# A gated linear recurrence and a cosine MLP on one core: every chunk in pairs, two tokens to a partition, and one written order of steps

## The chip, the cores and the metric

The kernel runs on one core of a Trainium2 chip. The metric is the device time of one execution in microseconds. Times given as a span come from one execution taken by the hardware profiler, from the first instruction to the last.

The engines: PE (TensorE) multiplies matrices into PSUM, eight banks of 512 float32 columns; DVE (VectorE), ACT (ScalarE) and POOL (GpSimd) work elementwise; SP (SyncE) issues DMAs, and ACT can as well. Each has its own queue and takes its instructions in order. They wait for one another by semaphores.

## The reference

```python
f = 1.0 / (1.0 + np.exp(-f_logit))              # B, H, S, D = 4, 8, 768, 48
state = np.zeros((B, H, D, D))
for t in range(S):
    state = f[:, :, t, :, None] * state + np.einsum('bhd,bhe->bhde', k[:, :, t], v[:, :, t])
    y[:, :, t] = np.einsum('bhd,bhde->bhe', q[:, :, t], state)
x = y.transpose(0, 2, 1, 3).reshape(B * S, H * D)       # 3072 x 384
h = x @ w_in                                    # w_in 384 x 2048
out = (h * np.cos(h)) @ w_out                   # w_out 2048 x 384
```

Inputs and output are float32.

## The kernel before

The 768 steps of a batch are cut into six chunks of 128 tokens, 24 chunks in all. Within a chunk the recurrence is written as masked attention; a state goes from chunk to chunk.

A chunk goes through these steps, which the text calls by these names. Loads of f, k, q and v (`load`, L396 and L399). *decay*: exp and log of f on ACT (L422, L437), running sums over the tokens on PE (L448 to L461), and their exponentials b and bi on ACT (L468). *Products* q b and k bi (L482, mostly POOL), v cast to bf16 (L389). Transposes of both products on PE (L511, L515) and their copy qkt out of PSUM (L525). *Scores* on PE (L541, L550), masked by DVE (am, L554). *Outer product* of keys and v on PE (L570, L575), added to the state by DVE (st, L584) and decayed (sz, L590). y from the state (L600) and from the scores (inner y, L607 and L612), copied out (yb, L525), transposed on PE (L630) and copied (xT, L525).

The MLP works on units of 128 or 256 tokens. *h* is x by w_in on PE (L651), into two banks; ACT takes the cosine (L658), DVE the product with h (gT, L661). *o* multiplies gT by w_out on PE in four quarters of four matmuls (L671), ACT or DVE copy the sum out (ot, L674), SP stores it (L682, L685). The weights come in by eight loads of 768 KB and are cast to bf16 (L389).

Exp and log are in one table of ACT, the cosine in another; ACT_TABLE_LOAD changes them (L737, L658). So decay is done for groups of chunks (`GROUPS`), seven in all.

The first four chunks (`NPAIR = 4`) are loaded as pairs of tokens: a partition takes tokens 2p and 2p+1, in pieces of 384 bytes, and two groups of four heads stand on the two halves of the partitions. The matmuls of these chunks take a form of their own (L448 to L454, L511, L541, L570, L607), in which a v padded with zeros (vp) keeps the halves apart. The other twenty put one token on a partition, in pieces of 192 bytes.

The order of the steps isn't written out. `Plan.run` takes every step with an assumed cost for each engine that may do it and a priority (`PR`), and puts next what can start first. It gives each step its engine, its buffer (`Slots`) and its banks (`Banks`): h may take banks 0 to 5, scores 2 to 7, single banks 2 to 7. A PSUM tile has two banks.

Of the kernel before, what the change touches and what calls it, by code (L numbers as in the profile page):

```python
# [9 lines left out]
F32 = mybir.dt.float32  # L10
# [3 lines left out]


class Slots:


    def __init__(self, aps, name):
        self.aps, self.name = aps, name  # L20
        self.free_at = [0.0] * len(aps)
        self.held = [False] * len(aps)
        self.last, self.now = [[] for _ in aps], [[] for _ in aps]

    def best(self):
        free = [(t, i) for i, t in enumerate(self.free_at) if not self.held[i]]
        return min(free) if free else None

    def take(self, i):
        self.held[i] = True  # L30
        self.last[i], self.now[i] = self.now[i], []

    def users(self, i):
        return self.last[i]

    def used(self, i, t, o):
        self.free_at[i] = max(self.free_at[i], t)
        self.now[i].append(o)

    def drop(self, i):  # L40
        self.held[i] = False

    def ap(self, i):
        return self.aps[i]


class Banks:


    def __init__(self, base, size, starts, name):  # L50
        self.base, self.size, self.starts, self.name = base, size, starts, name

    def best(self):
        b, out = self.base, None
        for k, s in enumerate(self.starts):
            r = range(s, s + self.size)
            if any(b["held"][i] for i in r):
                continue
            c = (max(b["free"][i] for i in r), k, s)
            if out is None or c < out:  # L60
                out = c
        return None if out is None else (out[0], out[2])

    def take(self, s):
        for i in range(s, s + self.size):
            self.base["held"][i] = True
            self.base["last"][i], self.base["now"][i] = self.base["now"][i], []

    def users(self, s):
        return sum((self.base["last"][i] for i in range(s, s + self.size)), [])  # L70

    def used(self, s, t, o):
        for i in range(s, s + self.size):
            self.base["free"][i] = max(self.base["free"][i], t)
            self.base["now"][i].append(o)

    def drop(self, s):
        for i in range(s, s + self.size):
            self.base["held"][i] = False

    def ap(self, s):
        t = self.base["tiles"][s // 2]
        return t if self.size == 2 else t[:, (s % 2) * 512:(s % 2) * 512 + 512]


class Val:


    def __init__(self, pool=None, ap=None):
        self.pool, self._ap, self.slot = pool, ap, None  # L90
        self.writers, self.uses, self.parts = [], 0, []
# [6 lines left out]
    @property  # L98
    def ap(self):
        return self._ap if self.pool is None else self.pool.ap(self.slot)  # L100


class Part:
    def __init__(self, whole, cut):
        self.whole, self.cut, self.writers = whole, cut, []
# [6 lines left out]
class Op:  # L112
    __slots__ = ("seq", "eng", "fn", "prio", "table", "deps", "vals", "alloc", "start", "end",
                 "lat", "waiting", "after", "grp", "dma", "name", "prior", "cost")


class Plan:


    SEM = 60.0  # L120
    PE_LAT = 180.0
    TABLE = 1290.0
    WINDOW = 60.0

    def __init__(self):
        self.ops = []

    def op(self, name, eng, fn, reads=(), writes=(), prio=0.0, table=None, lat=0.0, grp=None,
           dma=None):
        o = Op()  # L130
        o.name, o.eng, o.fn, o.prio, o.table = name, eng, fn, prio, table
        o.lat, o.grp, o.dma, o.prior = lat, grp, dma, []
        o.seq, o.deps, o.alloc, o.vals, o.after = len(self.ops), set(), [], [], []
        for v in reads:
            o.deps.update(v.writers)
            if isinstance(v, Val):
                for p in v.parts:
                    o.deps.update(p.writers)
        for v in writes:
            w = getattr(v, "whole", v)  # L140
            if w.pool is not None:
                o.alloc.append(w)
            if v.writers:
                o.deps.add(v.writers[-1])
        for v in list(reads) + list(writes):
            v = getattr(v, "whole", v)
            if v.pool is not None and v not in o.vals:
                o.vals.append(v)
                v.uses += 1
        for v in writes:  # L150
            v.writers.append(o)
        self.ops.append(o)
        return o

    def run(self):
        free = dict.fromkeys(("PE", "ACT", "DVE", "POOL", "SP"), 0.0)
        table, lock, bus, hot, pe_end = None, None, 0.0, 0.0, 0.0
        left = {}
        for o in self.ops:
            o.waiting = len(o.deps)  # L160
            for d in o.deps:
                d.after.append(o)
            if o.grp is not None:
                left[o.grp] = left.get(o.grp, 0) + 1
        ready = [o for o in self.ops if not o.waiting]
        order, n = [], len(self.ops)
        while len(order) < n:
            cand = []
            for o in ready:
                at, pe = 0.0, "PE" in o.eng  # L170
                for d in o.deps:
                    t = d.end + (0.0 if pe and d.eng == "PE" else self.SEM)
                    if pe and d.eng == "PE":
                        t = d.end - d.lat
                    at = max(at, t)
                ok = True
                for v in o.alloc:
                    if v.slot is not None:
                        continue
                    b = v.pool.best()  # L180
                    if b is None:
                        ok = False
                        break
                    at = max(at, b[0] + self.SEM)
                if not ok:
                    continue
                pick = None
                for e, cost in o.eng.items():
                    if e == "ACT" and lock is not None and o.grp != lock and o.table is not None:
                        continue  # L190
                    s = max(at, free[e])
                    sw = self.TABLE if e == "ACT" and o.table not in (None, table) else 0.0
                    if pick is None or s + cost + sw < pick[0]:
                        pick = (s + cost + sw, s, e, cost)
                if pick is not None:
                    cand.append((pick[1], o.prio, o.seq, o, pick[2], pick[3]))
            assert cand, "no op can be placed: " + str(
                [(o.name, o.prio, lock, o.grp, [v.pool.name for v in o.alloc]) for o in ready])
            first = min(cand, key=lambda c: c[:3])
            best = min((c for c in cand if c[4] == first[4] and c[0] <= first[0] + self.WINDOW),  # L200
                       key=lambda c: (c[1], c[0], c[2]))
            s, _, _, o, e, cost = best
            if e == "ACT" and o.table is not None:
                if o.table != table:
                    s += self.TABLE
                table = o.table
                if o.grp is not None:
                    left[o.grp] -= 1
                    lock = o.grp if left[o.grp] else None
            for v in o.alloc:  # L210
                if v.slot is None:
                    v.slot = v.pool.best()[1]
                    v.pool.take(v.slot)
                    o.prior += v.pool.users(v.slot)
            o.cost = cost
            if e == "PE":
                hot *= math.exp((pe_end - s) / 2500.0)
                if hot < 0.5:
                    cost *= 1.9
                hot = 1.0 - (1.0 - hot) * math.exp(-cost / 2500.0)  # L220
                pe_end = s + cost
            o.start = s
            free[e] = s + cost
            if o.dma is not None:
                bus = max(s + cost + 700.0, bus) + o.dma
                o.end = bus + 1250.0
            else:
                o.end = s + cost + (self.PE_LAT if e == "PE" else 55.0 if e in ("ACT", "DVE") else 0.0)
                o.lat = o.end - s - cost
# [20 lines left out]
NPAIR = 4  # L250
# [519 lines left out]
```

## Time and profile before

| | |
|---|---|
| time, median of 3 runs | 227.56 us (226.14 to 229.81) |
| profiled execution, span | 225.4 us |
| busy: PE, DVE, ACT, POOL | 187.4, 138.2, 137.8, 71.8 us |
| instructions of PE (matmuls) | 1976 |
| mean granted clock of TensorE | 0.970 |
| moved by DMA | 30.20 MB, mean 134 GB/s |
| packets under 512 B | 92480 of 99158 |

The profiled execution has no time of its own beside the runs; its span is 2.2 us below their median. A line of the profile names the line of the kernel, the engine and the operation, then what is written and read. Busy times of PE are of pipelined matmuls: one that lasts 0.33 us may be followed by another after 0.16. In rows of waits the numbers are microseconds in total, how often, and the longest.

### The profile page before, as it was taken

What the parts mean: (1) busy time and instruction counts of PE and PEld (TensorE: products, weight loads), DVE (VectorE), ACT (ScalarE), POOL (GpSimd) and SP (SyncE); (2) the same over time, 40 slices, a digit from 0 to 9 for tenths busy, and PEclk for the clock granted to TensorE, in tenths of its full rate; (3) what the DMA queues carried; (4) which work ended last, traced back from release to release, by engine and by line L of the source; (5) the groups of instructions that cost most, each with busy time, mean ns of one, the idle gap of its engine ahead of it and who ended that gap; (6) DMA issues with size and microseconds to landing.
All of it is one profiled execution on the core that took longest, in us unless ns stands there. A gap on an engine that the chain in (4) does not pass through costs nothing.

```text
span 225.4 us, 4908 instructions
## 1 busy us (share of the span) xinstructions
PE 187.4 (83%) x1976; PEld 140.9 (62%) x1976; DVE 138.2 (61%) x188; ACT 137.8 (61%) x165; POOL 71.8 (32%) x111
## 2 busy tenths in 40 slices
PE   0327876699999579799999898989999999998883
PEld 0215875476686458577778565666777786677551
DVE  1628568686739648748865326958878562673600
ACT  2545558845998675556366898438454478775401
POOL 8120142813081284460110065838321001600000
PEclk9999999679999958999999999999999999999999
DMA  6979899999989999995120189791010100111011
GB/s 185 171 201 346 163 199 226 334 284 183 204 181 188 193 202 201 190 217 101 49 59 35 41 177 219 164 192 57 1 38 0 45 28 0 47 60 38 0 66 73
DMA packets 99158, 30.20 MB, mean 134 GB/s; under 512 B 92480, under 2 KB 97600, under 8 KB 99136
## 3 DMA queue, kind: packets, MB, share of 16 engines
q1 hardware_dynamic: 98592, 29.70, 56.7%
q8 instruction: 15, 0.25, 0.4%
q10 hardware_dynamic: 544, 0.20, 0.4%
q14 instruction: 7, 0.06, 0.1%
HBM read 25.17 MB, written 4.72 MB: 133 GB/s over the span
## 4 chain that ended last, share of the span: by engine, by line
PE 58%; DVE 12%; ACT 6%; issue 5%; POOL 0%; DVEq 0%; ACTq 0%
PE ps L651 24%; PE ps L671 23%; PE ps L515 3%; PE ps L550 2%; DVE am L554 2%; DVE st L584 2%; ACT qkt L525 2%; PE ps L630 2%; DVE gT L661 2%; DVE qkt L525 2%; PE ps L612 1%; ACT cosh L658 1%; PE ps L600 1%; DVE yb L525 1%; DVE vb L389 1%
## 5 line engine op out<-in xcount | busy, mean ns | idle before, releaser
L671 PE MATMUL ps<-w_out_bf,gT 128*128 128x384 bf16 x384 | 71.3, 328 | 7.2 <-ACT qkt L525 2.5
L651 PE MATMUL ps<-xT,w_in_bf 128*128 128x256 bf16 (+1 forms) x624 | 74.5, 275 | 0.5 <-DVE xT L525 0.4
L661 DVE TENSOR_TENSOR gT<-ps,cosh 128x1024 bf16<-128x1024 f32 x48 | 58.3, 1221 | 18.2 <-ACT cosh L658 17.1
L658 ACT ACTIVATE cosh<-ps,halfpi 128x1024 bf16<-128x1024 f32 x48 | 53.0, 1113 | 23.8 <-PE ps L651 21.5
L651 PEld LDWEIGHTS <-w_in_bf 128*128 128x128 bf16 x624 | 59.1, 102 | 10.1 <-issue 1.0
L671 PEld LDWEIGHTS <-gT 128*128 128x128 bf16 x384 | 35.9, 98 | 29.2 <-issue 9.5
L482 POOL TENSOR_TENSOR qk<-q,b 128x384 bf16<-128x384 f32 x21 | 21.3, 1015 | 48.7 <-ACT b L468 22.8
L590 POOL TENSOR_TENSOR sz<-st,b 64x192 bf16<-64x192 f32 x32 | 16.3, 510 | 30.9 <-DVE st L584 27.8
L554 DVE TENSOR_TENSOR am<-ps,umask 128x1024 bf16<-128x1024 f32 x20 | 24.2, 1217 | 2.3 <-PE ps L550 1.5
L482 POOL TENSOR_TENSOR qk<-k,bi 128x384 bf16<-128x384 f32 x21 | 21.6, 1032 | 1.6 <-ACT bi L468 1.6
L674 ACT COPY ot<-ps 128x384 f32<-128x384 f32 x13 | 6.2, 479 | 16.4 <-PE ps L671 13.9
L468 ACT ACTIVATE b<-ps 128x776 f32<-128x776 f32 (+1 forms) x14 | 10.1, 729 | 9.6 <-PE ps L461 4.4
L584 DVE TENSOR_TENSOR st<-ps,sz 128x384 f32<-128x384 f32 x16 | 8.9, 556 | 11.1 <-issue 3.3
L525 DVE COPY qkt<-ps 128x1024 bf16<-128x1024 bf16 x15 | 10.3, 688 | 7.8 <-PE ps L575 2.7
L674 DVE COPY ot<-ps 128x384 f32<-128x384 f32 x11 | 6.0, 554 | 13.2 <-PE ps L671 9.8
L525 ACT COPY qkt<-ps 128x1024 bf16<-128x1024 bf16 x9 | 9.1, 1011 | 7.7 <-PE ps L515 5.4
L422 ACT ACTIVATE f<-f 128x768 f32<-128x768 f32 (+1 forms) x14 | 10.3, 747 | 5.1 <-DMA f<-in_f_logit_dram 5.0
L389 POOL CAST vb<-v 128x384 bf16<-128x384 f32 x10 | 5.0, 504 | 26.3 <-PE ps L612 18.5
L525 ACT CAST yb<-ps 128x384 bf16<-128x384 f32 x16 | 7.6, 476 | 9.4 <-PE ps L612 3.9
L515 PE MATMUL ps<-ident,qk 128*128 128x128 bf16 x160 | 12.7, 224 | 0.2 <-ACT ot L674 0.2
L630 PE MATMUL ps<-ident,yb 128*128 128x128 bf16 x72 | 8.8, 237 | 3.9 <-DVE ot L674 1.3
L515 PEld LDWEIGHTS <-qk 128*128 128x128 bf16 x160 | 10.7, 100 | 1.6
(69 smaller groups left out, 189.8 us busy)
## 6 DMA issues: line engine op xcount, KB each, us to landing
f<-in_f_logit_dram SPq DMA_DIRECT2D x20, 192.0 KB, 3.9
v<-in_v_dram SPq DMA_DIRECT2D x20, 192.0 KB, 3.7
k<-in_k_dram SPq DMA_DIRECT2D x20, 192.0 KB, 3.9
q<-in_q_dram SPq DMA_DIRECT2D x20, 192.0 KB, 3.7
out_dram<-ot SPq DMA_DIRECT2D x20, 192.0 KB, 1.9
gT<-in_moe_w_in_dram SPq DMA_DIRECT2D x4, 768.0 KB, 5.8
gT<-in_moe_w_out_dram SPq DMA_DIRECT2D x4, 768.0 KB, 7.6
f<-in_f_logit_dram SPq DMA_DIRECT2D x8, 96.0 KB, 5.4
```

The lines of the kernel that those rows point to most:

```text
L482: lambda e, j=j, src=src, dec=dec: E(e).tensor_mul(out=qk.ap[:, j, :, 0:D].rearrange("p (e h) d -> p h e d", e=2) if pm else qk.ap[:, j, : ...
L515: nc.tensor.transpose(out=o[:, j * NP + p, :], in_=pair(j, p), identity=ident)
L525: (nc.scalar.copy if e == "ACT" else nc.vector.tensor_copy)(out=o, in_=i_)
L554: P.op("am", {"DVE": dve(1024)}, lambda e: nc.vector.tensor_mul(out=am.ap.rearrange("p r a n -> p (r a n)").rearrange("p (a n) -> p a n", ...
L584: P.op("st", {"DVE": dve(384)}, lambda e: nc.vector.tensor_add(out=st.ap, in0=pv(), in1=S_in.ap), reads=[ps, S_in], writes=[st], prio=prio)
L590: eng().tensor_mul(out=S_out.ap[s, :, r, :], in0=srcap()[s, :, r, :], in1=bt.ap[s, i, HD:, None].broadcast_to([64, NP, D]))
L630: nc.tensor.transpose(out=pxv()[:, m, :], in_=yb.ap[:, m * 128:(m + 1) * 128], identity=ident)
L651: nc.tensor.matmul(ph.ap[:, g * T:(g + 1) * T], lhsT=w_in_bf[:, m, f0:f0 + 128], rhs=x[:, m, :], start=(g % (G // 2) == 0 and m == 0), sto ...
L658: nc.scalar.activation(out=co.ap, in_=ph.ap, func=AF.Sin, bias=halfpi),
L661: P.op("g", {"DVE": dve(1024)}, lambda e, ph=ph, co=co, gv=gv: nc.vector.tensor_mul(out=gv.ap, in0=ph.ap.rearrange("p (g t) -> p g t", t=T ...
L671: nc.tensor.matmul(po.ap[:, 0:d_model], lhsT=gT.ap[:, j, i * C:(i + 1) * C], rhs=w_out_bf[:, j, :], start=(j == 0), stop=(j == KF - 1))
L674: P.op("ot", {"ACT": act(384), "DVE": dve(384)}, lambda e, po=po, ot=ot: (nc.scalar.copy if e == "ACT" else nc.vector.tensor_copy)(out=ot. ...
```

## The change

All 24 chunks are now worked on as twelve pairs of 256 consecutive tokens of a batch. A partition takes tokens 2p and 2p+1 of the pair, so that a load is 128 partitions by eight heads by 384 bytes. Pair 0's loads of f, k and q are cut into two halves of heads, and pair 1's f, k and q too. The two chunks of a pair stand on the two halves of the partitions for the scores, the outer product and the inner y, which contract over 64 partitions; the zero-padded v is gone. The gate puts the tokens back in order, so that a store is of contiguous rows.

`describe` names every step; it no longer has costs or priorities. `ORDER` is one written list of all steps. Each word has the step's name, its engine (T PE, S ACT, V DVE, G POOL, Y SP) and the slots or banks that it writes. `emit` goes through it. `apart` tells the framework that two steps on different engines, which use different banks of one PSUM tile and share no buffer, don't depend on each other. Any step may use any bank. Buffers: qkt 5 for 3, am, sz and yb 4 for 3, 3 and 2, co 4 for 3, g 5 for 6; k, q and v three of a pair each for four of a chunk. Two of the loads were issued by ACT before, fourteen are now. There are 22 table loads for 14.

```diff
-GROUPS = [(1, 1, 1, 1), (2,), (2, 2), (2, 2), (2, 2), (2, 2), (2,)]
-NPAIR = 4
...
+HALVES = (0, 1)
+SLOTS = {"f": 3, "k": 3, "q": 3, "v": 3, "sp": 3, "b": 3, "bi": 3, "qk": 3, "vb": 3, "qkt": 5, "am": 4,
+         "sz": 4, "st": 2, "yb": 4, "x": 4, "g": 5, "co": 4, "ot": 4}
+ORDER = """
+zqk.1:V zsz.2:V f0.1:Y0 f0.0:S k0.0:Y0 q0.0:Y0 v0:S0 q0.1:S f1.1:Y1 zsp.2:V k0.1:Y ex0.1:S w0.2:Y0
+f1.0:Y ex0.0:S ln0.0:S2 vb0:V0 ln0.1:S cum0.1:T0 eb0.1:S0 k1.0:Y1 cum0.0:T1 eb0.0:S qm0.0:G1
...
+wc1.1:G h0.11:T tk1.1:T3 wc1.0:G h1.00:T4 co0.1:S1 sc1.0:T6 am1.0:V2 g0.1:V tq1.1:T h1.01:T
...
+g1.0:V3 h1.11:T y1.1:T6,7 w1.3:Y4 yi1.0:T k2:Y2 y1.0:T o0.1:T2 ex2:S yi1.1:T q2:Y2 zsz.3:G st1.1:V0
...
+"""
...
+        G.step(name, ("SP", "ACT"), lambda e: eng(e).dma_start(
+            out=val.ap.rearrange("p h e d -> p h (e d)"),
+            in_=tok.rearrange("h (p e) d -> p h (e d)", e=2)), writes=[val])
...
+        def outer(e, u):
+            for a in range(2):
+                for x in range(2):
+                    for g in gs:
+                        t = slice(64 * g, 64 * g + 64)
+                        i = 2 * u + a
+                        nc.tensor.matmul(ps[g].ap[:, 96 * i:96 * i + 96].rearrange("p (t n) -> p t n", t=2),
+                                         lhsT=qk.ap[t, u, 1, x, 2 * a:2 * a + 2, :].rearrange("p h d -> p (h d)"),
+                                         rhs=vb.ap[t, 2 * i:2 * i + 2, x, :],
...
+        def inner(e, u):
+            for h in range(4):
+                for x in range(2):
+                    for g in range(2):
+                        t = slice(64 * g, 64 * g + 64)
+                        i = 4 * u + h
+                        nc.tensor.matmul(py[g].ap[:, D * i:D * i + D], lhsT=am[u].ap[t, h % 2, h // 2 * 2 + x, :],
+                                         rhs=vb.ap[t, i, x, :], start=(py[g].first and h == 0 and x == 0),
...
+def apart(tc, users, s, e, made):
+    vals = [v.whole for v in s.reads + s.writes]
+    banks = {b for v in vals if isinstance(v.pool, Banks) for b in range(v.slot, v.slot + v.pool.size)}
+    places = {(v.pool.name, v.slot) for v in vals if v.pool is not None and not isinstance(v.pool, Banks)}
+    for t in {b // 2 for b in banks}:
+        for engine, others, theirs, there in users[t]:
+            if engine != e and not banks & theirs and not places & there:
+                for b in others:
+                    for a in made:
+                        tc.declare_no_dep(a, b, reason="the steps use different PSUM banks")
```

In `ORDER` f, k, q, v are loads, ex and ln the exp and log, cum the running sums, eb and ei their exponentials, qm and km the products, tq and tk the transposes, sc the scores, ps the outer product, y the inner y, yi the part from the state, tx and xe the output transposes and their copies, w and wc the loads and casts of weights, co and g the cosine and the gate.

## The prediction

> **What bounds the kernel now.** I read the page first, then the busy time by stretches, then TensorE's timeline, then the waits.
>
> From the page, the span, TensorE's busy time and the 40 slices of TensorE, its granted clock and the DMA engines:
>
> ```profile
> span 225.4 us, 4908 instructions
> ...
> PE 187.4 (83%) x1976; PEld 140.9 (62%) x1976; DVE 138.2 (61%) x188; ACT 137.8 (61%) x165; POOL 71.8 (32%) x111
> ...
> PE   0327876699999579799999898989999999998883
> PEclk9999999679999958999999999999999999999999
> DMA  6979899999989999995120189791010100111011
> ```
>
> TensorE (PE) is the fullest engine; nothing else passes 61%. But its first seven slices are thin, and from the eighth on it is nearly full. So the span is a start in which PE waits for loads and for the serial steps of the first chunks, and then a dense stage that PE's own work sets. The rows by stretch (us, length, then busy time and count of PE, weight loads, DVE, ACT, POOL; clock; DMA share; GB/s) put numbers to it:
>
> ```profile
> 40.00:45.00 5.00, 3.35 (x24) 2.06 (x25) 3.27 (x5) 4.85 (x5) 4.18 (x5) 0.66 1.13 327
> ...
> 80.00:90.00 10.00, 8.94 (x88) 7.37 (x88) 6.80 (x10) 6.56 (x8) 6.98 (x9) 0.70 0.98 199
> ...
> 8.00:15.00 7.00, 2.96 (x25) 2.14 (x24) 1.71 (x10) 4.91 (x12) 0.59 (x2) 1.00 0.67 152
> 52.00:64.00 12.00, 11.58 (x124) 7.69 (x122) 8.05 (x13) 9.42 (x13) 2.68 (x5) 1.00 1.03 204
> 15.00:22.00 7.00, 3.42 (x50) 2.79 (x51) 5.12 (x9) 2.65 (x2) 1.37 (x2) 1.00 0.96 338
> ```
>
> The dense stage begins where PE gets its first 256-token unit, and the short matmuls of attention can be priced by the distance between starts in the timeline (start, length; a length includes the drain, the distance doesn't):
>
> ```profile
> 31.57 0.42 PE L541 MATMUL ps<-qkt 48*64 48x128 bf16 x16 [0.83 <-ACT bi L468]
> 31.98 1.50 PE L651 MATMUL ps<-xT,w_in_bf 128*128 128x128 bf16 x24
> ...
> 44.06 4.92 PE L651 MATMUL ps<-xT,w_in_bf 128*128 128x256 bf16 x24
> ...
> 109.81 0.40 PE L550 MATMUL ps<-qkt 48*128 48x128 bf16 x8
> 110.14 0.37 PE L612 MATMUL ps<-vb,am 128*128 128x48 bf16 x8
> 110.36 0.33 PE L575 MATMUL ps<-vb,qk 128*128 128x96 bf16 x4
> 110.52 0.82 PE L651 MATMUL ps<-xT,w_in_bf 128*128 128x256 bf16 x6
> ```
>
> Dense from 44.06, then. By such distances and the chain's pieces, an h matmul of 256 columns takes 109 ns (12 in 1.31), an o matmul 163 ns (4 in 0.65). All of h and o is 528 x 0.109 + 96 x 0.0625 + 384 x 0.163 = 126.1 us. A plain chunk costs: running sums 0.28, transposes 0.45, scores 0.33, inner y 0.21, state part of y 0.17, outer product 0.17, output transposes 0.17: 1.78. The four paired ones cost 2.32 each. Less what the first and last chunks of a batch lack, attention is 43.4, all of PE 169.5 us at full clock. Some 16.3 of it is done by 44.06; the other 153.2 take until the last matmul at 222, 178 us. So 25 us of the dense stage are waits and half clock. What PE waited for after 40 us:
>
> ```profile
> PE ps L671 <- ACT qkt L525: 2.5, 3, 1.1
> PE ps L630 <- DVE ot L674: 1.3, 1, 1.3
> PE ps L671 <- ACT ot L674: 1.1, 2, 0.6
> ```
>
> None of these three reads what its releaser wrote: an o matmul has no use for a copied qkt. They are waits for a PSUM bank, or for the other bank of the same two-bank tile. The list's rows of that sort sum to 10.8 us; true reads (yb, am, qkt, xT, w_out) are some 4.
>
> **The change, part by part.** The sum goes against the profiled execution, span 225.4; the median of the three runs, 227.56, is 2.2 above it, and I add 2.2 at the end.
>
> *The start.* Before, the first load issued is a 768 KB weight, and the first exp runs at 7.69 us; afterwards pair 0's f goes first, in halves on SP and ACT. With 384-byte pieces I take 227 GB/s (152 at a share of 0.67, above) and for weights 350 (338 at 0.96). So f (0.39 MB) is there at about 4.5, two exps and two logs at 0.52 end at 6.6, the sums (0.75 each at the start's pace) and four exponentials at 0.5 at 9.7, POOL's and DVE's products at 11, transposes and qkt (1.01) at 12.1, scores and masks (1.21 each) at 15.3, y, yb, output transpose and x at 17.5: the first h then, where before it was 25.2. POOL's four casts of w_in (1.46 each) stand in its queue between; the last is done near 22.7, and each late one holds the h behind it. The second pair's x then sets the dense start. q's second half stands on SP behind all of w_in, and o0.1 stands in PE's queue ahead of it, with w_out's first quarter: 7.08 MB in all, 3.14 at 227 and 3.93 at 350, 25 us after a start at 2, landed at 28, cast at 29.6. Then y, yb, transposes, x: h of the first 256-token unit near 32.4. That is 11.7 earlier at about the same work done. Bounds: if the DMA engines give only the 213 GB/s which the first seven slices average before, the gain is 6.5; with no delay in queues 13. I take -11.7.
>
> *PE's added work.* Matmuls go from 1976 to 2448. For 20 chunks: the sums take the paired form, 0.44 for 0.28 (L448 to L454 at 28.70 to 29.14); scores 0.41 for 0.33 (L541 above); inner y has 16 of half depth for 8, and L541's 25.6 ns apiece as the floor gives 0.41, against 0.21 if halves of the array overlap fully; the outer product 8 for 4, 0.21, at most 0.34. A chunk becomes 2.26, bounds 2.01 and 2.38. 20 x (2.26 - 1.78) = +9.6 (bounds +4.7, +12.1). All on the path, since PE sets the stage. I take the middle by L541, the nearest row.
>
> *Bank waits.* Steps in different banks of a tile are declared independent, and every step has its bank written out. The two ot waits at the tail (0.56 each) go for sure; others may be true reuse. In the built program o matmuls that wait on ACT fall from 13 to 3, but all waiting PE instructions only from 253 to 246. -6 of 10.8 (bounds 0 and -10.8).
>
> *Loads.* Inputs from chunk 4 on go in 384-byte pieces: 227 against 198 GB/s (204 at 1.03). One 3.1 us piece of the chain at 93 hangs on a v load; -2 (bounds 0, -3.1). The Trainium skill, "DMA: Bandwidth & Descriptors", Specifications, puts the line rate at pieces of 512 B and more; by it neither size reaches the line rate and this term would be 0.
>
> *Clock.* The rows at 0.66 and 0.70 lose 3.4 and 3.0 us. The ramp stays, the second follows idle time that partly goes: -3 (bounds 0, -6.4).
>
> *ACT.* The table loads go from 14 to 22: 8 x 1.283 = +10.3 us; DMA issues on ACT from 2 to 14, 12 x 0.69 = +8.3 (two took 1.37). Three w_in casts (4.4) and four yb go to others. ACT becomes 146 plus 10 of issues, DVE about 152 (13 more qk products at 0.55, 18 sz, 8 fewer vb), POOL about 60. All lie beside PE's 179; 0 on the path, and +10.3 if the cover goes: behind a table load stand the cosines, and for a cosine waits an h bank. The timeline of ACT shows how much a switch takes:
>
> ```profile
> 34.50 1.11 ACT L658 ACTIVATE cosh<-ps,halfpi 128x1024 bf16<-128x1024 f32 x1
> 35.64 1.28 ACT L737 ACT_TABLE_LOAD   x1
> 36.93 0.84 ACT L422 ACTIVATE f<-f 128x768 f32<-128x768 f32 x1
> ```
>
> The load starts 0.03 after the cosine ends, and exp follows at once. The Trainium skill, "ScalarE: Activation LUTs", What ACT_TABLE_LOAD costs, counts 1.38 us of drain besides, 2.66 per switch; by that the eight would add 21.3 us of ACT. It speaks against more, shorter exp blocks, but the rows here show no such gap.
>
> *Stores and SP.* 28 stores become 24, all contiguous, and SP issues 72 DMAs for 146; SP's waits were on ot, nothing on the path: 0. The gate writes its product reordered, still 48 at 1.22.
>
> The sum: 225.4 - 11.7 + 9.6 - 6 - 2 - 3 = 212.3 of span, 214.5 us. All good ends: 225.4 - 13 + 4.7 - 10.8 - 3.1 - 6.4 = 196.8, so 199. All bad: 225.4 - 6.5 + 12.1 + 10.3 = 241.3, so 243.5.
>
> **Rivals.** *ACT becomes the gate.* An exp block is two table loads and four passes, 2 x 1.28 + 4 x 0.83 = 5.9 us without a cosine; there are eleven. Against: before, with seven, all h groups together idled 0.5 us. For: ACT now also issues loads, and a full ring has held SP 5.1 us for two of them. If the blocks outlast the o quarters set beside them, the eight loads' 10.3 fall on the path, and stalls and clock give nothing back: 225.4 - 11.7 + 9.6 + 10.3 = 233.6, so 236. It decides once h waits on cosines for more than some 8 us. *The start is given back.* Half-depth matmuls at the high bound, bank waits mostly true, the second pair later: 225.4 - 9 + 12.1 - 3 = 225.5, so 228. For: only seven waits fewer. *More than forecast.* Row groups overlap and the bank waits go: 225.4 - 13 + 4.7 - 10.8 - 3.1 = 203.2, so 205.
>
> **How the numbers follow.** Forecast 0.60, more than forecast 0.08, given back 0.15, ACT the gate 0.17. Two per cent, about what a measurement of this kernel tells from no change, is 223.0 to 232.1. So faster 0.68, same 0.15, slower 0.17. The range goes from 201, between the third rival and the good ends, to 235, just short of the second side's 236: about 0.06 and 0.13 left out.
>
> **What would show it.** Right: the first 256-column h near 32; PE's matmul work near 179 at full clock; inner y at 0.4 per chunk; o waiting on ACT under 1 us; 22 table loads at 1.28 with no gap. Wrong: h groups waiting on cosines; first h after 22; PE's slices no fuller than 0.9 after the start; the DMA engines no faster with 384 bytes than with 192.

## The result and the profile after

The changed kernel takes 210.66 us, the median of four runs (210.62 to 210.75), against 228.61 of four runs of the kernel before (226.14 to 229.81). The ratio is 0.931, with a 95% interval of 0.925 to 0.937; it is taken over the fast runs alone, and two of the four of before, 229.65 and 229.81, lie over 1.5% above their fastest. The profiled execution took 210.67 us with a span of 208.9, so 1.8 us lie around the span. From the page of the changed kernel, the same rows that were shown of before:

```profile
span 208.9 us, 5682 instructions
...
PE 189.6 (91%) x2448; PEld 140.1 (67%) x2448; DVE 153.7 (74%) x216; ACT 141.3 (68%) x166; POOL 60.1 (29%) x72
...
PE   0487786999999999999999999999998899999993
PEclk9999999999999999999999999999999999999999
DMA  6999999989993457770960192803320000030112
```

From the eighth slice on only two are under 0.9 for TensorE, and the last; before there were ten, scattered, and the last. No slice of this execution has a low granted clock. DVE and ACT have become busier, as the change makes them.

The timeline of PE (start, length, last in brackets the idle time and its releaser) shows the two marks of the start, the first h and the first h of 256 columns:

```profile
19.11 1.44 PE L517 MATMUL ps<-x,w_in_bf 128*128 128x128 bf16 x12
...
36.57 2.78 PE L517 MATMUL ps<-x,w_in_bf 128*128 128x256 bf16 x24 [0.94 <-DVE x L190]
...
198.18 7.31 PE L533 MATMUL ps<-w_out_bf,g 128*128 128x384 bf16 x44
```

Before, the dense stage ran from 44.06 to 221.92 (the last o, 218.51 + 3.41), 177.9 us. Now it runs from 36.57 to 205.49, 168.9 us. The start gives 7.5 us, the dense stage 9.0: together the 16.5 us of span. And yet PE has more to do. What PE waits for after 40 us, the whole list (total us, times, longest):

```profile
PE ps L517 <- DVE g L499: 1.2, 2, 1.0
PE ps L398 <- DVE g L499: 0.4, 1, 0.4
PE ps L517 <- ACT x L190: 0.3, 1, 0.3
PE ps L378 <- DVE qk L350: 0.2, 1, 0.2
```

That is 2.1 us, where the same list of before sums to 14.9. Not one o matmul (L533) waits. Every row here is a true read, or a step that takes over a bank which the gate or a copy has to leave first.

The prices of PE's new work are read from pieces of the chain of waits (start, length, what; a length here is the distance to the next piece):

```profile
126.79 0.51 PE ps L459 x32
...
132.47 0.35 PE ps L398 x16
...
135.33 1.31 PE ps L517 x12
```

The 32 half-depth matmuls of the inner y of a whole pair take 0.51 us, 16 ns apiece on average; twelve h matmuls 1.31, as before. With the sums at 0.43, transposes 0.45, scores 0.35, inner y 0.25 (0.31 where half a pair's stand by themselves, as in 14 of 17 places), state part 0.17, outer product 0.24 (0.28 in most places) and output transposes 0.17, a chunk costs 2.06 to 2.16 where a plain one cost 1.78. One price is not in these pieces. The timeline of PE:

```profile
127.23 0.82 PE L533 MATMUL ps<-w_out_bf,g 128*128 128x384 bf16 x4
127.89 0.33 PE L469 MATMUL ps<-sz,qkt 128*128 128x96 bf16 x4
128.06 0.81 PE L533 MATMUL ps<-w_out_bf,g 128*128 128x384 bf16 x4
128.81 0.34 PE L419 MATMUL ps<-vb,qk 64*128 64x96 bf16 x4
```

From start to start, four o matmuls take 0.66 us when the next matmul uses the whole depth of the array (L469), and 0.75 when it uses half of it (L419). The same 0.10 us more stands wherever a group of scores, outer products or inner y follows matmuls of the whole depth, 54 times in the dense stage; before, only the scores were so, 20 times. If every matmul of the dense stage is counted with the distance that is usual between its kind and the next one's, PE's work there is by this estimate 164.1 us of the 168.9, so 4.8 are lost; before it was 155.2 of 177.9, with 22.7 lost.

So the account is: start -7.5, PE's work +8.9, lost time in the dense stage -17.9, in all the measured -16.5. The lost time is what is left over of the stage, not a sum of its own.

### The profile page after: what moved, and what is told of

It reads as the page before. It is cut to its first block, busy times and chain, and to the rows that moved or that the text cites. A ratio compares the mean times of both kernels' runs of the same rounds, so it can differ in the third digit from the quotient of the medians.

```text
span 208.9 us, 5682 instructions
## 1 busy us (share of the span) xinstructions
PE 189.6 (91%) x2448; PEld 140.1 (67%) x2448; DVE 153.7 (74%) x216; ACT 141.3 (68%) x166; POOL 60.1 (29%) x72
## 4 chain that ended last, share of the span: by engine, by line
PE 77%; DVE 8%; ACT 6%; DMA 5%; issue 2%; DVEq 0%; ACTq 0%
PE ps L533 29%; PE ps L517 25%; PE ps L378 5%; PE ps L398 4%; DMA k<-in_k_dram 3%; DVE g L499 3%; PE ps L459 3%; PE ps L419 3%; PE ps L322 2%; PE ps L469 2%; PE ps L491 2%; DMA f<-in_f_logit_dram 2%; DVE qk L350 2%; DVE am L402 2%; ACT L522 1%
## 5 line engine op out<-in xcount | busy, mean ns | idle before, releaser
L499 DVE TENSOR_TENSOR g<-ps,co 128x1024 bf16<-128x1024 f32 x48 | 61.8, 1305 | 19.4 <-ACT co L522 18.3
L517 PE MATMUL ps<-x,w_in_bf 128*128 128x256 bf16 (+1 forms) x624 | 72.0, 268 | 2.6 <-DVE g L499 1.4
L533 PE MATMUL ps<-w_out_bf,g 128*128 128x384 bf16 x384 | 73.3, 327 | 0.0
L522 ACT ACTIVATE co<-ps,halfpi 128x1024 bf16<-128x1024 f32 x48 | 52.9, 1114 | 23.0 <-PE ps L517 21.6
L533 PEld LDWEIGHTS <-g 128*128 128x128 bf16 x384 | 33.8, 98 | 18.9 <-DVE g L499 0.2
L402 DVE TENSOR_TENSOR am<-ps,pmask 128x1024 bf16<-128x1024 f32 x24 | 28.8, 1217 | 2.9 <-PE ps L398 2.6
L350 POOL TENSOR_TENSOR qk<-k,bi 128x384 bf16<-128x384 f32 x14 | 15.5, 1118 | 24.0 <-ACT bi L341 21.8
L442 POOL TENSOR_TENSOR sz<-st,b 64x192 bf16<-64x192 f32 x14 | 8.5, 610 | 30.3 <-DVE st L435 29.9
L322 PE MATMUL ps<-sp,incl 128*128 128x384 bf16 x24 | 8.5, 356 | 7.0 <-ACT sp L311 6.1
L190 ACT CAST yb<-ps 128x384 bf16<-128x384 f32 x12 | 5.5, 476 | 13.2 <-PE ps L469 11.1
L398 PE MATMUL ps<-qkt 48*64 48x128 bf16 x384 | 10.5, 229 | 1.5 <-DVE g L499 0.5
L190 POOL CAST vb<-v 128x768 bf16<-128x768 f32 x10 | 8.5, 856 | 9.5 <-DMA v<-in_v_dram 9.4
```

The lines of the kernel that those rows point to most:

```text
L190: (nc.scalar.copy if e == "ACT" else eng(e).tensor_copy)(out=o, in_=i)
L322: nc.tensor.matmul(o4, lhsT=incl, rhs=w[:, 0:1, :, 0:D].broadcast_to([128, 2, 4, D]), start=True, stop=False)
L350: G.step(f"{nm}{n}.{u}", ("POOL", "DVE"), lambda e, u=u, j=j, src=src, dec=dec: eng(e).tensor_mul(out=qkp[u][j].ap[:, :, :, 0:D], in0=swap ...
L398: nc.tensor.matmul(o[t, r, 2 * a + x, :].rearrange("p (e n) -> p e n", e=2), lhsT=qkv(u)[s, 1, a, g, x, :], rhs=qkv(u)[s, 0, a, g, :, :], ...
L402: G.step(f"am{n}.{u}", ("DVE",), lambda e, u=u, sc=sc: nc.vector.tensor_mul(out=am[u].ap.rearrange("p r b n -> p (r b n)").rearrange("p (y ...
L499: nc.vector.tensor_mul(out=o.rearrange("p b (n e) -> p b e n", e=2), in0=ph.ap.rearrange("p (b e n) -> p b e n", e=2, n=64), in1=co.ap.rea ...
```

## The experiments

A PSUM tile has two banks; without a declaration, a step that uses one bank of a tile is made to wait for earlier steps on the other. In the first expectations below, Theory 1 is the prediction's view: the declarations remove a part of the bank waits, some 6 to 10 us, and the rest of the gain comes from the start, the pairs and the order. Theory 2 is the rival: a written order with chosen banks avoids such waits by itself, and the declarations add next to nothing.

### The declarations taken out of the changed kernel, and put into the kernel before

a_no_apart is the changed kernel with one line less:

```diff
         made = (nc.find_inst_by_name(f"I-{i}") for i in range(n0 + 1, nc.next_id()))
-        apart(tc, users, s, e, [i for i in made if i is not None])
```

> The changed kernel with the same order, engines and banks, but without the declarations that steps in different banks of a PSUM tile are independent. Theory 1 (the dense stage got shorter because waits for the other bank of a tile are gone): PE's waits on DVE and ACT copies come back, 6 to 10 us, time 217 to 221. Theory 2 (the written order, the free choice of banks and the extra buffers keep such waits off PE by themselves): 211 to 213.

It took 243.73 us (242.52 to 243.91), ratio to before 1.073 (1.064 to 1.081). Both theories were far too low: without the one line the changed kernel is 33 us slower than with it, and slower than the kernel before. The dense stage starts at 42.64 us instead of 36.57 and lasts 25.8 longer. The list of PE's waits after 40 us sums to 21.9 us, where the changed kernel's sums to 2.1:

```profile
PE ps L533 <- DVE qkt L190: 5.6, 3, 2.4
PE ps L398 <- ACT qkt L190: 1.8, 1, 1.8
...
PE ps L533 <- ACT qkt L190: 1.2, 1, 1.2
...
PE ps L533 <- DVE st L435: 1.1, 2, 0.7
```

An o matmul (L533) reads gates and w_out, never qkt or a state. These are the rows that the kernel before had at L671, and they are larger here: `ORDER` puts any step into any bank, while the planner before kept h to banks 0 to 5 and scores and single banks to 2 to 7. That the free placing is why they are larger was not tested by itself.

b_apart is the kernel before, with its planner and its order untouched, and only the declarations added:

```diff
+            n0 = nc.next_id()
             o.fn(o.eng)
+            made = (nc.find_inst_by_name(f"I-{i}") for i in range(n0 + 1, nc.next_id()))
+            apart(tc, users, o, [i for i in made if i is not None])
```

> The kernel before, with its planner and order unchanged, and only these declarations added. Theory 1: 6 to 10 us of PE's waits go, and with them the half-clock stretch near 80 us; 217 to 222, two thirds of the whole gain. Theory 2: the planner's order stalls for other reasons; 225 to 229.

It took 211.90 us (211.27 to 215.28), ratio 0.932 (0.920 to 0.944). That is nearly the whole result, from some fifteen lines that change no arithmetic, no order, no engine and no load. The declarations are worth more than either theory gave them: 16 us in the old order, 33 in the new one. The dense stage of b_apart even starts later than before, as the timeline shows, with the wait that is left:

```profile
43.56 1.44 PE L671 MATMUL ps<-w_out_bf,gT 128*128 128x384 bf16 x4 [4.03 <-DVE w_out_bf L389]
44.80 4.08 PE L651 MATMUL ps<-xT,w_in_bf 128*128 128x256 bf16 x24
```

From 44.80 to its last matmul at 206.71 are 161.9 us, 16.0 less than before. PE's work in it, counted as above, is the same: 155.3 us for 155.2. The lost time falls from 22.7 to 6.6.

### Which direction of the waits counts

A declaration can free a step of PE from a copy in the neighbour bank, or free a copy, cosine or gate from PE's matmuls, or another engine's copy, in the neighbour bank. The prediction counted only the first, since only PE was full. b_pe and b_copies declare one direction each:

```diff
-            if engine != o.eng and not banks & theirs and not places & there:
+            if o.eng == "PE" and engine != o.eng and not banks & theirs and not places & there:   # b_pe
+            if o.eng != "PE" and engine != o.eng and not banks & theirs and not places & there:   # b_copies
```

> The kernel before with the declarations added only where the later step is PE's (PE needn't wait for ACT's or DVE's work in the other bank of a tile). With all declarations it took 211.9 for 228. If the cost was PE's own waits for the neighbour bank, as the trace's list of PE's waits names them (10.8 us): 213 to 218. If it was mostly copies and cosines that waited for matmuls in the neighbour bank: 222 to 227.

> The complement: declarations only where the later step is ACT's or DVE's (a copy, cosine or mask needn't wait for PE's work in the other bank). If the cost was PE's own waits: 224 to 228. If it was late copies and cosines, which then hold PE: 213 to 219. If both are needed, both kernels stay over 219.

b_pe took 216.96 us (216.72 to 219.65; ratio 0.959, 0.949 to 0.968), b_copies 216.77 (215.91 to 217.47; 0.954, 0.945 to 0.963), against 227.73 of before in the same runs. b_pe's -10.8 equals the sum of the bank rows in before's list of PE's waits, 10.8 us, but the equality is partly chance: b_pe's list still sums to 8.9 us against 14.9, since some 2 us of these rows are still there and the wait for w_out has grown from 0.7 to 2.6. The lost time of the dense stage as a whole, with waits too short for the list and the time at a low clock, falls from 22.7 to 11.4 us. b_copies' -11.0 was to be seen too, in the lists of ACT's and DVE's waits of the kernel before, which were not read for the prediction because idle time of an engine with room to spare looked harmless. From ACT's list of before:

```profile
ACT yb L525 <- DVE st L584: 2.4, 2, 1.7
ACT qkt L525 <- PE ps L671: 2.3, 3, 0.9
...
ACT ot L674 <- DVE qkt L525: 1.8, 2, 0.9
```

and from DVE's:

```profile
DVE ot L674 <- PE ps L515: 3.3, 1, 3.3
DVE qkt L525 <- PE ps L575: 2.7, 1, 2.7
DVE st L584 <- ACT qkt L525: 2.7, 2, 1.7
...
DVE qkt L525 <- PE ps L671: 1.7, 3, 0.8
```

A copy of transposes has no use for an o matmul (L671), a copy of an o sum none for transposes (L515). These seven rows sum to 16.9 us. b_pe still has them, at 13.8 us; in b_copies and b_apart none of them is in the lists. Such idle time isn't harmless: without these rows the kernel is 11.0 us faster. The likely way is that the copy that waits is what PE's next step reads, and that it holds a bank meanwhile; no run follows a single copy. The two directions add to 21.8 us alone and give 16.2 together, so they overlap.

### What the rest of the change is worth

Given the declarations, pairs and written order bring 211.90 to 210.66. That 1.2 us is hardly more than three of b_apart's runs differ among themselves (0.8; the fourth took 215.28). It is a difference of large parts: the dense stage begins 8.2 us earlier (36.57 for 44.80) and lasts 7.0 longer (168.9 for 161.9), since PE has 8.8 more to do (164.1 for 155.3) and loses 1.8 less (4.8 for 6.6).

*Loads in smaller pieces.* d_192 loads the two tokens of a partition by two DMAs of 192-byte pieces each:

```diff
-        G.step(name, ("SP", "ACT"), lambda e: eng(e).dma_start(
-            out=val.ap.rearrange("p h e d -> p h (e d)"),
-            in_=tok.rearrange("h (p e) d -> p h (e d)", e=2)), writes=[val])
+        def two(e):
+            for x in range(2):
+                eng(e).dma_start(out=val.ap[:, :, x, :], in_=tok.rearrange("h (p e) d -> p h e d", e=2)[:, :, x, :])
+        G.step(name, ("SP", "ACT"), two, writes=[val])
```

> The changed kernel with each input load cut into two DMAs, one per token of the pair, so that pieces are 192 bytes instead of 384; same bytes, order and places. If the size of the pieces matters for the start: the 3.1 MB of inputs ahead of the dense stage go at some 198 for 227 GB/s, 2 us later, and the dense stage follows: 212 to 214. If the engines' work hides it: 210 to 211.5. Rival (loads are near the bound all through): 216 and more.

It took 216.11 us (215.65 to 216.84), 5.5 more. Nearly all of it is in the start: the first 256-column h is at 42.10 instead of 36.57. The rates in the same stretch, 44 to 56 us, for the changed kernel and then for d_192 (the last three columns are clock, DMA share and GB/s):

```profile
44.00:56.00 12.00, 12.00 (x181) 8.26 (x180) 11.05 (x19) 9.11 (x11) 5.56 (x6) 1.00 1.20 268
```

```profile
44.00:56.00 12.00, 12.00 (x132) 8.36 (x130) 10.76 (x12) 9.71 (x10) 3.57 (x6) 1.00 1.11 223
```

No weights are loaded in this stretch, so 384-byte pieces, with a few stores, move at 268 GB/s and 192-byte ones at 223. But the experiment changed a second thing: it doubled the DMA issues, and those on ACT stand ahead of ACT's first work. ACT's timeline of d_192:

```profile
4.64 2.51 ACTq L278 DMA_DIRECT2D q<-in_q_dram  x2
7.19 1.28 ACT L573 ACT_TABLE_LOAD   x1 [7.19 <-DMA v<-in_v_dram]
8.48 0.94 ACT L309 ACTIVATE f<-f 128x384 f32<-128x384 f32 x2
```

and of the changed kernel:

```profile
2.49 1.28 ACT L572 ACT_TABLE_LOAD   x1 [2.49 <-issue]
4.14 0.94 ACT L308 ACTIVATE f<-f 128x384 f32<-128x384 f32 x2 [0.37 <-DMA f<-in_f_logit_dram]
```

The first exp is 4.3 us later, since ACT's queue was held by its own issues. So most of the 5.5 us can be the issues, and how much the piece size is worth stays open: between nothing and 5.5 us.

*Loads of the second pair.* In the changed kernel's start the longest piece of the chain after the first loads is a half of pair 1's k, which ACT issues:

```profile
16.59 7.24 DMA k<-in_k_dram
```

g_early0 issues it and the other late half, of q, on SP, ahead of the third load of w_in:

```diff
-sc0.1:T6 am0.1:V1 w0.0:Y2 wc0.2:G q1.0:S1 cum1.0:T1 wc0.1:G ei1.0:S1 km1.0:V1 w0.3:Y3 y0.0:T0,3
-y0.1:T yb0.0:S0 ln1.1:S wc0.0:G tk1.0:T2 k1.1:S v1:Y1 tx0.0:T0 xe0.0:S0 yi0.1:T sz0.11:G2 wc0.3:G
+sc0.1:T6 am0.1:V1 q1.0:Y1 k1.1:Y w0.0:Y2 wc0.2:G cum1.0:T1 wc0.1:G ei1.0:S1 km1.0:V1 w0.3:Y3 y0.0:T0,3
+y0.1:T yb0.0:S0 ln1.1:S wc0.0:G tk1.0:T2 v1:Y1 tx0.0:T0 xe0.0:S0 yi0.1:T sz0.11:G2 wc0.3:G
```

> The changed kernel with the second halves of q and k of pair 1 taken from ACT's queue (issued at 13.1 and 16.6, landed at 21.9 and 23.9) and put on SP ahead of the third quarter of w_in. Theory (the dense stage waits for these two loads): they land near 15, the second pair's x is there 2 to 4 us earlier, 207 to 209.5; the quarter of w_in that comes 1.7 us later costs no more than 1. Rival (something else, w_out's first quarter or the casts, comes next at once): 210 to 211.5.

It took 210.70 us, no change, and the first 256-column h is at 36.59. The wait for k is gone and another has its place, a quarter of w_in and its cast. The chain of g_early0:

```profile
12.48 9.84 DMA g<-in_moe_w_in_dram
...
22.44 1.48 POOL w_in_bf L190
...
23.96 0.84 PE ps L517 x12
```

So the order of these loads only chose which is late.

*Loads on ACT.* h_sp gives the loads that ACT issues from pair 2 on, nine by the list of steps, to SP (`f2:S2` becomes `f2:Y2`, and so k3, v4, k10, v5, k7, f9, f10 and f11).

> The changed kernel with the ten loads from pair 2 on that ACT issues given to SP, at the same places of the list. Theory (PE sets the pace, ACT is nearly as full): ACT is relieved of ten issues of 0.4 to 0.5 us, three quarters of which reached the path when ACT was loaded more, but SP's queue holds them behind other loads and stores: 207.5 to 211.5. Rival (SP, blocked for 13 us by the w_out loads, brings pair 2 late): 212 and more.

210.77 us, no change: after the start these issues cost ACT's queue nothing that reaches PE.

*Table loads.* e_tables puts two more table loads into every second exp block (32 instead of 22, with a one-column cosine between); e_none takes exp in place of the cosine, which computes another function but needs one table load in all.

```diff
+                if blocks % 2 == 0:
+                    nc.scalar.activation(out=tiny, in_=tiny, func=AF.Sin)
+                    nc.scalar.preload_act_table_set("natural_log_exp_and_others")
```

```diff
-                out=co.ap, in_=ph.ap, func=AF.Sin, bias=halfpi), reads=[ph], writes=[co], table="S")
+                out=co.ap, in_=ph.ap, func=AF.Exp, bias=halfpi), reads=[ph], writes=[co], table="E")
```

> The changed kernel with ten more table loads (32 for 22): in every second exp block a one-column sine and a second load of the exp table. ACT gets 10 x 1.283 plus 5 x 0.2 = 13.9 us more. Theory (PE sets the pace, ACT's blocks lie beside it with little to spare): a third or less reaches the path, 211.5 to 215.5. Rival (ACT is the gate): nearly all of it, 221 to 225.

> The changed kernel with exp in the place of the cosine, in the table that exp and log use already: another function of h is computed, and of the 22 table loads one stays. ACT loses 27 us of table loads and nothing else. Theory (PE's work sets the dense stage, ten more loads cost three quarters of their time because they stood in single lumps): 204 to 208. Rival (ACT's table loads are on the path at three quarters of their time all through): 188 to 195. If they are hidden: 209.5 and more.

e_tables took 221.11 us (220.29 to 221.65), 10.4 more for 13.2 us more of ACT (154.5 for 141.3). e_none took 208.38, 2.3 less for 27.2 us less of ACT (114.1). So the 22 loads are hidden but for 2.3 us, and there is no room for more: of the next ones four fifths reach the end. Of these 10.4 us, 1.9 are a later dense start (38.46), and the profiled execution has a low clock in places (0.68 in 35 to 40 us), so not all of it need be ACT's queue. In e_tables' list of PE's waits what ends ACT's longer queue shows:

```profile
PE ps L517 <- DVE g L499: 2.9, 3, 1.6
PE ps L419 <- ACT ot L190: 1.6, 1, 1.6
```

*PE's work.* f_twice does every output transpose twice, 72 more matmuls at 56 ns, 4.0 us:

```diff
-                for m in range(KM):
+                for m in 2 * list(range(KM)):
```

> The changed kernel with every output transpose done twice (72 more matmuls on PE of 56 ns, 4.0 us, same result). Theory (PE's own work sets the dense stage): 3.2 to 4.2 us longer, 213.9 to 214.9. Rival (PE is full by the page but other engines' latencies set the pace): under 1.5 us, below 212.2.

213.48 us (213.40 to 213.66), 2.8 more: 70% of added PE work reaches the end. 0.7 of the 4.0 us fall ahead of the dense stage, which begins no later (36.55); of the 3.3 in it, 2.8 reach the end. PE's work is the bound there.

*The start of b_apart.* i_early_wout takes b_apart and moves the load of w_out's first quarter ahead of five loads of chunks 4 and 5, and that of the second quarter up by two, to remove the wait of 4.0 us and the half clock after it:

```diff
+MOVED = (("w10", "k5"), ("w11", "k4"))
...
+    for name, ahead in MOVED:
+        op = order.pop(place(name))
+        order.insert(place(ahead), op)
```

> The kernel before with all declarations (211.9), and two loads moved in SP's list: the first quarter of w_out from behind five loads of chunks 4 and 5 to ahead of them, the second two loads up. All other queues as they were. In the trace with declarations, PE stands 4.03 us at 43.56 for that quarter's cast, with x of the next unit behind the cast on DVE, and the stage starts at half clock. Theory (this load's place is all that is late there): the cast at 39.5, the first 256-column h near 41.5, 3 to 5 us less, 206.5 to 209, below the changed kernel's 210.7. Rival (the five loads, 2.2 us later, hold chunks 4 and 5 in turn): 211 to 214.

212.39 us (210.99 to 214.52), ratio 0.935 (0.930 to 0.941): no gain over b_apart, and not better than the changed kernel. The wait falls to 0.6 us and the first 256-column h comes at 40.62, 4.2 earlier; but inputs of chunks 4 and 5 are late: POOL's product waits 2.7 us for a load of q, until 43.96. Busy PE by stretch (length, PE first, clock third from the end) in b_apart:

```profile
44.00:54.00 10.00, 9.25 (x79) 6.75 (x77) 8.07 (x8) 5.05 (x5) 1.67 (x2) 0.83 1.04 266
...
74.00:84.00 10.00, 7.63 (x112) 5.97 (x109) 8.27 (x14) 8.36 (x12) 7.97 (x11) 1.00 0.96 194
```

and in i_early_wout:

```profile
44.00:54.00 10.00, 7.58 (x77) 5.53 (x75) 6.88 (x7) 4.70 (x5) 6.26 (x7) 1.00 0.95 249
...
74.00:84.00 10.00, 8.87 (x96) 6.81 (x97) 6.52 (x11) 7.80 (x10) 6.73 (x8) 0.66 1.01 199
```

The gap moved from 40 to 44 into 44 to 54, and the low clock from the first of these stretches to the last.

*The pairs alone.* c_pairs sets `NPAIR = 24` in the kernel before, with six vp buffers.

> The kernel before with all 24 chunks in its paired form (NPAIR = 24, buffers for the padded v 6 for 3), order by its planner as before. Theory (PE sets the dense stage, the paired form costs PE 0.28 to 0.5 us per chunk): 20 chunks add 5.6 to 10 us, 233 to 238. Rival (192-byte pieces on the DMA engines set the pace up to 100 us): 384-byte pieces give back 3 us or more, 221 to 226.

It took 275.49 us, but what its steps compute changed too, in a part that wasn't traced, so this is no price of the paired form. That price without the new order stays open.

## Why the prediction was right, and where it was not

The forecast was 214.5 us in a range of 201 to 235, the measurement 210.66. The direction and the size hold. Of the terms, PE's added work came out near its size; the start brought 4.2 us less than forecast and the lost time of the dense stage 6.9 more, and these two errors partly cancel.

*The start: -11.7 forecast, -7.5 measured.* The first h came at 19.11 for 17.5, and the dense stage at 36.57 for 32.4. The step that failed is "Then y, yb, transposes, x". The loads that it starts from were nearly right: w_out's first quarter was there at 27.3 (forecast 28) and cast at 28.8 (29.6), and the last input of the second pair, a half of k, had landed at 23.8. But from the cast to the h of 256 columns are 7.8 us where the forecast had 2.8. The chain of waits names what lies between, among it a gate, 24 h matmuls of the unit before, and the copies yb:

```profile
28.13 1.23 DVE g L499
29.40 1.50 PE ps L517 x24
...
32.76 0.87 ACT yb L190 x2
```

g_early0 agrees: the late halves earlier, the h at 36.59. Which of these steps sets 36.57 was not separated.

*PE's added work: +9.6 forecast, +8.9 measured in the dense stage.* The size was right by two errors that cancel. The floor of 25.6 ns, taken from L541 for half-depth matmuls, was too high: the inner y takes 0.25 to 0.31 a chunk, not 0.41, and the scores 0.35, not 0.41. L541's matmuls stand in the two halves of the array too, but have 128 columns each, where the inner y has 48. On the other side the 0.10 us ahead of each half-depth group had no term; 34 more of them are 3.3 us. The outer product took mostly 0.28, not 0.21. f_twice confirms that such a term goes mostly to the end.

*Waits, loads and clock: -6, -2 and -3 forecast, -17.9 measured together.* "-6 of 10.8" was the mis-sized term, for two reasons. The declarations of PE's side alone brought 10.8 us (b_pe). And the same false waits on ACT and DVE, worth 11.0 alone, were left out, since the forecast followed only what PE waits for by name. The count that argued for caution, waiting PE instructions 253 before and 246 after, says nothing: the number of waits doesn't tell how long they last. That the total came out so near is partly luck. Without the -6 the forecast's sum would be 220.5 us, and without the declarations the changed kernel takes 243.73: the forecast didn't see that the new order brings many more false waits, nor that the declarations take these away too.

*Clock.* The dips at 40 to 50 and 80 to 90 (0.66 and 0.70) are gone in the profiled execution of the changed kernel, without anything done to them by itself. Its three other runs have a mean granted clock of 0.989 to 0.990 and take the same time within 0.1 us. In b_apart the second dip is gone (1.00 in 74 to 84), while the first is still there beside its w_out wait (0.83). The dips that are shown here stand beside idle time of PE, but not all idle time has one: in those 74 to 84 us PE is busy for only 7.63. What the clock gave by itself no run shows.

*Loads.* 227 GB/s for 384-byte pieces was too low: 268 in 44 to 56 us and 262 in 5.0 to 8.6. The rate came from a stretch of before with 152 GB/s at a DMA share of 0.67; dividing by the share didn't give the full rate. The Trainium skill, "DMA: Bandwidth & Descriptors", Specifications, puts the line rate at pieces of 512 bytes and more; below it, by these runs, 384 bytes are still some 1.2 times as fast as 192. What the term of -2 was worth by itself no run shows.

*ACT.* 22 table loads of 1.283 us, and the next operation follows within 0.03:

```profile
109.91 1.11 ACT L522 ACTIVATE co<-ps,halfpi 128x1024 bf16<-128x1024 f32 x1 [0.20 <-PE ps L517]
111.04 1.28 ACT L572 ACT_TABLE_LOAD   x1
112.34 0.81 ACT L341 ACTIVATE bi<-ps 128x768 f32<-128x768 f32 x1
```

The 1.38 us of drain which the Trainium skill, "ScalarE: Activation LUTs", What ACT_TABLE_LOAD costs, adds per switch isn't there. ACT on the path was put at 0 and is 2.3 (e_none). The rival "ACT becomes the gate" was wrong as the kernel stands and right in its slope: e_tables.

*DVE.* "Still 48 at 1.22" was wrong; what that did to the end was not tested. The groups of the page (count, then busy us, mean ns, and idle before) give the gate 1305 ns for 1221, 48 times, 4.0 us:

```profile
L499 DVE TENSOR_TENSOR g<-ps,co 128x1024 bf16<-128x1024 f32 x48 | 61.8, 1305 | 19.4 <-ACT co L522 18.3
...
L533 PE MATMUL ps<-w_out_bf,g 128*128 128x384 bf16 x384 | 73.3, 327 | 0.0
```

The second row is one of the forecast's own marks: o waits for nothing at all (before 7.2 us).

The rival "the start is given back" (228 us) didn't come; "more than forecast" (205 us) was right in that the bank waits go, and missed by its start (it had -13, measured are -7.5) and by PE's work (it had +4.7, measured are +8.9).

What stays open: the 4.8 us that the dense stage still loses, of which its list of waits names 2.1, and the price of each step between the last load and the dense start.

## What to carry to other kernels

Where a tile holds several banks that different steps use, look through the waits of every engine for rows whose releaser wrote nothing that the waiting step reads; sum them, and declare the steps independent before anything else is rebuilt: here that alone brought the kernel before 16.2 us. Do this for the engines with room to spare too: their waits alone were worth 11.0 us. A new order can bring such waits of its own: here the one line was worth 33 us in it. Where matmuls of half depth take turns with others, count the turns: each cost 0.10 us here. The Trainium skill, "Perfetto Trace Analysis", Matmuls, advises to rotate independent matmul groups through the banks so that copies overlap the next group; the runs here show that rotation alone can leave the order serial (243.7 us), and that it pays once the framework knows the banks as separate (210.7).

## What the runs showed of the hardware

Matmuls of 64 rows and 48 columns in the two halves of the array take 16 ns apiece on average (32 in 0.51 us), and 19 ns in groups of 16 (0.31). The Trainium skill, "TensorE: Matmul & The Clock Gate", section "Wait — 56ns, not 53.3ns?", states a floor of about 25 ns for any small matmul; the single-group ones of before agree (eight in 0.21, 26 ns), the row-grouped ones don't, and by that floor the inner y of a pair would have taken an estimated 0.80 us.

A matmul that uses the whole depth of the array is followed 0.10 us later than usual when the next uses half of it: four o matmuls take 0.66 us ahead of L469 and 0.75 ahead of L419.

Pieces of 384 bytes moved at 262 to 268 GB/s (changed kernel, 5.0 to 8.6 and 44 to 56 us) and of 192 bytes at 223 to 226 (d_192, 44 to 56 and 5 to 10 us), at a DMA share above 1.1 in both.

A DMA issue on ACT is not free: one takes 0.48 to 0.60 us of its queue in the first microseconds of the changed kernel, and two of them 2.51 in d_192 from 4.64 on, when many loads are under way, and what stands behind waits.

The gate's product, written in another order of tokens, took 1305 ns for 1221 with the same operands and count.
